# Three of batch 0's activation blocks on GpSimd, and the first batch's loads and products in smaller pieces

## The chip, the cores and the metric

The kernel runs on one core of a Trainium2 chip. Its engines work side by side, each through its own queue in order: TensorE (PE, with its weight loads PEld), VectorE (DVE), ScalarE (ACT), GpSimd (POOL) and SyncE (SP), whose queue issues transfers. GpSimd and ScalarE issue transfers too. The metric is the device time of one execution in microseconds (us).

## The reference

For each of 8 batches and 8 heads, 512 tokens `x` and 32 states `state` of width 64 attend to each other, both ways. The rows of both, heads side by side, then go through a two-layer network with a parametric ReLU:

```python
scores = scale * np.matmul(x, state.transpose(0, 1, 3, 2))
...
xread = np.matmul(a, state)
scores2 = scale * np.matmul(state, x.transpose(0, 1, 3, 2))
...
sread = np.matmul(a2, x)
return np.concatenate([xread, sread], axis=2).astype(np.float32)

h = x @ w_in
g = np.maximum(h, 0.0) + alpha * np.minimum(h, 0.0)
return (g @ w_out).astype(np.float32)
```

`a` and `a2` are softmaxes of the scores. There are 4352 rows, 512 wide; the hidden width is 2048.

## The kernel before

The token rows never form `xread`. A batch's states are multiplied by `w_in` first (`state_w_in`, token `m.b.f`, one for each quarter f of the hidden width, copied to fp16 by `mo`), and the softmax weights of the batch, transposed, then multiply that product: `first` (L562, token `F.b.jc.k`) makes one block of 128 hidden units by 512 tokens of `h` in PSUM bank k with two matmuls, one for each group g of four heads. `negative` (L618, `N`) writes relu(-h) to SBUF on ScalarE, and `prelu` (L623, `G`) makes the fp16 activation from it and from h, which is still in PSUM, on VectorE: neg * (1 - alpha) + h. Sixteen such blocks make a batch. Numbers 0 to 7 are the token rows of the batches, 8 all state rows together.

Batch 0 then takes the second product directly (`second`, L631, `S.b.q.jc2`: two hidden blocks at a time into the bank of token quarter q, drained by `O`). Batches 1 to 8 take one step of a Strassen scheme: seven products `P.b.p.i.c` (L718) of 4 matmuls per piece, on sums of activations (`U`, L694) and of weights (`W`, L676, needed once), drained by `K` (L737) and `Q` (L752). Most U and all W run on GpSimd ("p" at the end of a token; "a" is ScalarE, "v" VectorE).

Batches 1 to 7 get their weights from scores for all 512 tokens in one two-bank PSUM tile (`sc`, also used by whole m products), a block transpose (`sb`), a maximum (`smax`), a shift on GpSimd (`ssh.p`), an exponential on ScalarE (`sexp`), a sum (`ssum`), a product with the reciprocal (`snorm`) and a transpose back (`wb`, L413). The same scores feed the other direction: maximum (`tm`), shift (`nb`), exponentials (`te`), a transposing transfer (`tt`) and reads (`rd`). Batch 0 is taken another way at the start, when nothing else is there: x comes in two fp32 loads on the SP queue (`load_x0`, L164), one for each group of four heads, and is cast (`x0_cast`, L174, `cx.j.g`), transposed on TensorE (`xt.0.j.g.k`, L296), copied out (`xo.0.j.g`, L304) and multiplied with the states into token-major scores (`token_scores`, L350, `tsc.j.g`); j is the half of the tokens. Maximum, shift, exponential, sum and norm follow for each group, then transposes on TensorE (`at`) and copies (`ao`) to the weights.

Nothing is scheduled by a compiler. The string `ORDER` (L17) is a list of tokens, `name.arguments`, and the loop at L778 calls them one after another. The order on each engine is the order of its tokens, and semaphores between the engines follow from the tiles. A bank number in a token fixes what has to be drained before. `Z.k.n` fills TensorE's queue with n matmuls on a pattern. `wi`, `wo`, `lx`, `lst` issue the loads of weights, x and states from GpSimd's queue; `xd` and `tt` issue transposing transfers from SP's.

## Time and profile before

| | |
|---|---|
| time, median of 3 runs (lowest to highest) | 209.35 us (209.3 to 209.4) |
| the profiled execution, its time | 209.3 us |
| the profiled execution, its span in the trace | 207.2 us |
| granted TensorE clock | 1.0 throughout |
| matmuls of first products, batches 0 to 7 (L568) | 256 |
| matmuls of Strassen products (L726) | 840 |
| activation blocks on VectorE (L624), 128x512 and 128x256 | 128 and 16 |

The span runs from the first to the last record of the trace; the time contains 2.1 us around it. Rows of the profile give a line of the kernel, an engine, an operation, what it writes and reads, and its shape. In rows of the timeline the first number is the start, the second the length, in us from the span's start; "xN" merges N instructions. A matmul's length is modelled, and it overlaps the next one's. What stands in brackets is the idle time ahead on that engine and who ended it.

### The profile page before, as it was taken

To read this page: it belongs to the slowest core of one execution; us is meant where nothing else is said; L and a number is where in the kernel's file an instruction comes from. 1 tells how busy PE (TensorE), PEld (TensorE's weight loads), DVE (VectorE), ACT (ScalarE), POOL (GpSimd) and SP (SyncE) were. 2 spreads that over 40 slices of the span, in tenths; PEclk is the share of its full clock that TensorE was granted. 3 is DMA by queue.
4 is the path that set the end of the run, shared out by engine and by line. 5 is a ranking of instruction groups with operands and counts; after the bars stand their busy time and mean duration, and the time that the engine had idled before them with its cause. 6 is when DMAs were issued, how large, how long until landed. Compare 5 with 4: busy or idle time off the path is not lost.

```text
span 207.2 us, 5043 instructions
## 1 busy us (share of the span) xinstructions
PE 198.9 (96%) x2003; PEld 131.7 (64%) x2003; DVE 182.6 (88%) x277; ACT 148.7 (72%) x298; POOL 144.0 (70%) x87
## 2 busy tenths in 40 slices
...
GB/s 178 223 204 204 206 202 184 116 126 198 92 155 166 175 221 179 38 79 135 252 97 131 214 17 51 55 54 103 0 0 99 6 101 54 0 51 74 48 136 152
DMA packets 45943, 24.74 MB, mean 119 GB/s; under 512 B 24288, under 2 KB 45408, under 8 KB 45920
## 3 DMA queue, kind: packets, MB, share of 16 engines
...
q0 software_dynamic: 12688, 8.62, 29.2%
q8 instruction: 15, 0.25, 0.5%
q10 hardware_dynamic: 272, 0.07, 0.1%
q14 instruction: 8, 0.07, 0.1%
...
## 4 chain that ended last, share of the span: by engine, by line
PE 81%; DVE 14%; issue 1%; DMA 1%; ACT 1%; POOL 0%; DVEq 0%; POOLq 0%; ACTq 0%
PE px L726 23%; PE h L568 23%; PE pv L726 12%; DVE g L624 7%; PE py L726 6%; PE o L638 6%; PE h L577 3%; PE m_ps L519 3%; PE fill L230 2%; DVE mx L381 1%; PE sr_ps L469 1%; DVE r L402 1%; DMA out_dram<-oq 1%; PE sc L316 1%; DVE ts L386 1%
## 5 line engine op out<-in xcount | busy, mean ns | idle before, releaser
L624 DVE SCALAR_TENSOR_TENSOR g<-neg,oma_sb,h 128x512 f16<-128x512 f32 (+1 forms) x144 | 94.5, 710 | 4.3 <-ACT neg L621 3.5
L621 ACT ACTIVATE neg<-h 128x512 f32<-128x512 f32 (+1 forms) x144 | 76.1, 590 | 14.0 <-PE h L568 8.2
L568 PE MATMUL h<-aT,m 128*128 128x512 f16 x256 | 64.5, 379 | 0.7 <-DVE g L624 0.5
L726 PEld LDWEIGHTS <-gsum 128*128 128x128 f16 x480 | 46.6, 98 | 9.6 <-issue 1.0
L568 PEld LDWEIGHTS <-m 128*128 128x128 f16 x256 | 24.1, 98 | 25.1 <-issue 4.3
L726 PEld LDWEIGHTS <-g 128*128 128x128 f16 x360 | 34.9, 98 | 7.3 <-issue 0.9
L705 POOL TENSOR_TENSOR gsum<-g 128x1024 f16<-128x1024 f16 (+1 forms) x14 | 28.7, 2060 | 14.4 <-PE pv L726 14.3
L705 POOL TENSOR_TENSOR gsum<-g,g 128x1024 f16<-128x1024 f16 x11 | 23.4, 2129 | 13.2 <-DVE g L624 13.1
L726 PE MATMUL px<-ws,gsum 128*128 128x256 f16 x240 | 29.8, 273 | 0.0
L742 ACT COPY kept<-px 128x512 f32<-128x512 f32 (+1 forms) x21 | 12.2, 582 | 23.8 <-PE px L726 22.8
L705 POOL TENSOR_TENSOR gsum<-gsum,g 128x1024 f16<-128x1024 f16 x11 | 23.4, 2126 | 3.4 <-DVE gsum L705 2.7
L705 POOL TENSOR_TENSOR gsum<-g,gsum 128x1024 f16<-128x1024 f16 x11 | 23.4, 2131 | 0.3
L545 ACT CAST m<-m_ps 128x512 f16<-128x512 f32 x36 | 19.9, 622 | 2.8 <-PE m_ps L519 2.7
L386 POOL TENSOR_TENSOR ts<-ts,mx 128x1024 f32<-128x1024 f32 x7 | 13.4, 1916 | 9.3 <-DVE mx L381 8.8
L638 PE MATMUL o<-w_out_sb,g 128*128 128x512 f16 x64 | 16.5, 379 | 0.0
L759 DVE TENSOR_TENSOR oq<-pv,kept 128x512 f32<-128x512 f32 (+1 forms) x16 | 10.5, 653 | 6.7 <-ACT kept L742 4.4
L726 PE MATMUL px<-w_out_sb,g 128*128 128x256 f16 x120 | 16.1, 273 | 0.0
L726 PE MATMUL px<-w_out_sb,gsum 128*128 128x256 f16 x120 | 16.1, 273 | 0.0
L726 PE MATMUL py<-w_out_sb,g 128*128 128x256 f16 x120 | 16.1, 273 | 0.0
L726 PE MATMUL pv<-ws,gsum 128*128 128x256 f16 x120 | 15.7, 273 | 0.0
L726 PE MATMUL pv<-ws,g 128*128 128x256 f16 x120 | 15.6, 273 | 0.0
L543 ACT CAST m<-m_ps 128x1024 f16<-128x1024 f32 x12 | 12.5, 1042 | 1.7 <-PE m_ps L519 1.6
...
## 6 DMA issues: line engine op xcount, KB each, us to landing
...
```

The costliest lines, as they stand in the source:

```text
L386: engine(e).tensor_tensor(blocks(cols(live["ts", b], j, S)), blocks(scored(b, j)), over_blocks(cols(live["mx", b], j, S // N)), ALU.subtract,)
L519: nc.tensor.matmul(t[N * k : N * (k + 1), :], st_head(b, h)[64 * r : 64 * r + 64, :], w_in_sb[64 * r : 64 * r + 64, c, 512 * f : 512 * (f ...
L543: copier(e)(m_tile(b, f), t)
L545: copier(e)(m_tile(b, f)[:, g, :], t[g])
L568: nc.tensor.matmul(h.rearrange("p (r j s) -> p r j s", r=2, j=2), ms[b, f][:, g, 128 * j : 128 * (j + 1)], weights(b, g), start=(g == 0), ...
L621: nc.scalar.activation(neg, h, RELU, bias=0.0, scale=-1.0)
L624: nc.vector.scalar_tensor_tensor(g_tile(b, jc), negs.pop((b, jc)), oma_sb[:, jc : jc + 1], hs.pop((b, jc)), ALU.mult, ALU.add,)
L638: nc.tensor.matmul(outs[b, q], g_tile(b, jc)[:, 128 * q : 128 * (q + 1)], w_out_sb[:, jc, :], start=not begun and jc == 2 * jc2, stop=left ...
L705: engine(e).tensor_tensor(t, x(), y(), op)
L726: nc.tensor.matmul(pbanks[b, name][:, i, :], of(b, c)[:, j, 128 * i : 128 * (i + 1)], moving[:, 4 * c + j, :], start=not begun and j == 0, ...
L742: copier(e)(t, pbanks[b, "x"])
L759: nc.vector.tensor_tensor(osb, pbanks[b, name], kept[b, add], ALU.add)
```

## The change

x of batch 0 comes in four loads of two heads each (pairs 0 to 3), three on the SP queue and one, pair 2, on ScalarE's, behind the first states' load, which is now issued first. Their fp32 tiles lie in the ring of buffers "osb" (4 of them). `x0_cast(i, g)`, the transposes, their copies and `token_scores(i, g)` take the pair i of group g with all 512 tokens, where they took one half j of the tokens for all four heads of the group; the number of casts, transposes, copies and score matmuls is the same.

`first_of_group` (token `A.b.jc.g.k`) is one of the two matmuls of `first`; sixteen of them replace `F` for the blocks 0 to 7 of batch 0, each pair starting with the group that its token names first. `kept_h` (`C`) copies h from PSUM to SBUF as fp32 on ScalarE, and `prelu_pool` (`H`) makes the activation from the copy on GpSimd with two operations, min(h, 0) * (1 - alpha) and h minus that. Both tiles come from the ring "osb". C and H replace N and G for batch 0's blocks 5, 8 and 11; the other 141 blocks keep N and G.

The whole order is new. Counted over it: 50 of the U's stand on GpSimd (47 before) and 14 on VectorE (17); all K's are on ScalarE (three were on VectorE); one state read is left on VectorE (four before); the shifts nb of batches 1 and 7 go from ScalarE to VectorE and that of batch 5 the other way; one part of the first states' copy and one copy of transposed x more, and one copy of m more, are on VectorE. The nine fills at the start become seven, and the fill at the very end is gone from there. Tokens of the order are shown up to the middle of batch 0 and at the end.

```diff
 ORDER = """
-stc.0.a stt.0.1 sbd.0.a cx.0.0.v lst xt.0.0.0.2 cx.1.0.v sbd.1.a xt.0.1.0.3 xo.0.0.0.a tsc.0.0.4 xo.0.1.0.v tsc.1.0
-cx.1.1.v Z.5.1 smax.0.0 xt.0.1.1.0 xo.0.1.1.v cx.0.1.a xt.0.0.1.2 ssh.v.0.0 sto.0.a Z.3.1 tsc.1.1.5 xo.0.0.1.a tsc.0.1
-m.0.0.1.3 sexp.0.0 mo.0.0.a.1 Z.0.1 smax.0.1 ssh.v.0.1 sexp.0.1 wi.1 str.0.2 wi.2 sro.0.a ssum.0.0 lx.1 snorm.p.0.0
-str.1.4 wi.3 sro.1.a ssum.0.1 oma Z.0.1 snorm.v.0.1 wo.1 Z.3.1 Z.5.1 m.0.1.0.3 mo.0.1.a.0 at.0.5 mo.0.1.a.1 at.1.2
-ao.0.v wo.0 ao.1.v mo.0.0.a.0 m.1.0 mo.1.0.v F.0.7.4 N.0.7 G.0.7 F.0.6.0 F.0.2.5 N.0.6 F.0.1.3 G.0.6 N.0.2 m.2.2.2.1
-N.0.1 mo.2.2.v.0 G.0.1 m.1.1 mo.1.1.a F.0.5.4 G.0.2 F.0.4.0 N.0.4 Z.2.1 N.0.5 m.0.2 mo.0.2.a F.0.3.2 F.0.0.3 N.0.0
-G.0.4 G.0.5 Z.5.1 xt.1.1.1.0 xo.1.1.1.v G.0.0 N.0.3 G.0.3 F.0.8.5 N.0.8 xt.1.0.1.4 xo.1.0.1.a wo.2 lx.2 F.0.9.0 N.0.9
-m.0.3 xt.1.1.0.3 G.0.8 xo.1.1.0.v xt.1.0.0.4 xo.1.0.0.v mo.0.3.a mo.2.2.a.1 Z.2.1 m.3.3.2.5 mo.3.3.a.0 sc.1 m.2.0.3.4
-mo.2.0.a.0 mo.2.0.a.1 G.0.9 wo.3 mo.3.3.a.1 F.0.11.1 S.0.1.3.0 sb.1 smax.1 ssh.p.1 S.0.2.3.2 m.2.3.3.4 mo.2.3.a.0
-N.0.11 W.1.0.p F.0.10.5 S.0.1.2 tm.1 S.0.2.2 G.0.11 N.0.10 G.0.10 F.0.12.3 W.1.1.p mo.2.3.a.1 S.0.1.0 F.0.14.4 N.0.12
-G.0.12 nb.1.a sexp.1 F.0.15.1 ssum.1.5 te.1.1 te.1.0 F.0.13.3 N.0.13 tsum.1 S.0.2.1 snorm.v.1 S.0.1.5 S.0.1.4 N.0.15
-m.1.3 mo.1.3.a S.0.1.1 wb.1 G.0.15 S.0.2.5 N.0.14 G.0.14 S.0.2.4 m.1.2 mo.1.2.a G.0.13 S.0.2.0 F.1.1.5 N.1.1 F.1.13.1
...
-U.7.3.1.v K.8.1.v P.7.7.0.1 P.7.7.1.1 U.8.1.0.v U.8.2.0.v K.7.4.a P.7.3.0.0 P.6.3.0.1 U.8.1.1.v P.8.7.0.0.0 Q.7.1.1
-P.7.4.1.0 P.7.4.1.1 P.7.4.0.0 U.7.4.1.v P.7.4.0.1 U.8.2.1.v P.8.6.0.1 Q.7.1.0 P.8.6.0.0 K.8.2.v P.7.3.1.0 P.7.3.1.1
-U.8.4.0.v U.8.3.1.v Q.6.0.1.a P.8.5.0.1 P.8.5.0.0 K.8.4.a P.8.7.0.1 Q.8.1.1 P.8.2.0.1 Q.8.0.0 P.7.3.0.1 U.8.4.1.v
-P.8.4.0.0 P.8.4.0.1 P.8.3.0.0 Q.7.0.1.a Q.8.1.0 P.8.3.0.1 Q.8.0.1.a Z.1.1
+Z.1.1 lst stc.0.a cx.0.0.v xt.0.0.0.2 stt.0.3 xo.0.0.0.v cx.1.0.a xt.0.1.0.4 sbd.1.v cx.1.1.v xt.0.1.1.5 cx.0.1.a
+xt.0.0.1.0 sbd.0.a wi.1 sto.0.a tsc.0.0.1 xo.0.1.1.a xo.0.1.0.v tsc.1.0 Z.2.1 smax.0.0 Z.3.1 ssh.v.0.0 xo.0.0.1.a
+tsc.1.1.4 sexp.0.0 tsc.0.1 smax.0.1 ssh.v.0.1 lx.1 Z.5.1 m.0.0.2.3 mo.0.0.a.0 Z.0.1 str.1.5 mo.0.0.a.1 str.0.1 Z.0.1
+Z.2.1 wi.2 ssum.0.0 sexp.0.1 Z.4.1 sro.0.a snorm.p.0.0 at.0.3 sro.1.a ssum.0.1 wi.3 m.0.1.0.2 mo.0.1.a.1 snorm.v.0.1
+at.1.4 wo.1 ao.0.v ao.1.v m.4.0.1.5 mo.0.1.v.0 wo.0 m.1.1 mo.4.0.a.1 A.0.3.0.3 mo.4.0.a.0 A.0.1.1.2 A.0.1.0 A.0.2.1.4
+mo.1.1.v A.0.2.0 wo.2 N.0.2 A.0.3.1 N.0.3 lx.2 A.0.5.0.5 A.0.5.1 C.0.5 m.1.0 mo.1.0.a oma G.0.2 H.0.5 xt.1.0.0.0 Z.1.1
+xt.1.0.1.1 G.0.3 A.0.0.1.4 N.0.1 xt.1.1.1.5 xo.1.1.1.v A.0.7.0.3 A.0.7.1 N.0.7 A.0.0.0 N.0.0 A.0.4.1.5 xo.1.0.1.v
+G.0.1 wo.3 m.0.2 G.0.7 xo.1.0.0.v A.0.4.0 N.0.4 G.0.4 mo.0.2.a xt.1.1.0.1 xo.1.1.0.v A.0.6.0.2 m.2.0.3.0 A.0.6.1 N.0.6
+mo.2.0.v.0 m.0.3 mo.0.3.a G.0.6 F.0.11.5 C.0.11 H.0.11 mo.2.0.a.1 xd.2 F.0.8.1 sc.1 m.2.3.3.2 mo.2.3.a.0 C.0.8
+mo.2.3.a.1 G.0.0 sb.1 F.0.10.4 smax.1 S.0.2.2.5 tm.1 m.2.2.0.3 mo.2.2.a.0 S.0.2.3 F.0.15.1 mo.2.2.a.1 F.0.9.2 F.0.13.0
+ssh.p.1 nb.1.v S.0.2.0 N.0.15 G.0.15 S.0.1.1.3 N.0.9 N.0.10 G.0.9 S.0.1.0 S.0.1.2 Z.1.1 sexp.1 G.0.10 ssum.1.2
+snorm.v.1 te.1.0 S.0.1.3 F.0.12.1 F.0.14.4 N.0.13 N.0.14 te.1.1 tt.1 S.0.2.5 S.0.1.5 H.0.8 S.0.2.4 S.0.1.4 G.0.14
+m.1.3 wb.1 S.0.2.1 N.0.12 G.0.12 mo.1.3.a m.3.3.2.4 mo.3.3.a.1 G.0.13 m.1.2 W.3.0.p mo.3.3.a.0 F.1.15.4 N.1.15 G.1.15
+tsum.1 F.1.14.2 N.1.14 G.1.14 F.1.1.1 N.1.1 F.1.0.0 S.0.1.6 G.1.1 F.1.6.4 N.1.0 G.1.0 N.1.6 S.0.2.6 G.1.6 F.1.13.2
...
+P.7.4.1.0 N.8.12 P.7.4.0.1 P.7.4.1.1 U.8.3.1.p P.7.3.1.1 N.8.15 G.8.12 G.8.15 U.8.1.1.v U.8.2.1.v P.7.4.0.0 U.8.2.0.v
+Q.7.1.0 K.8.1.a P.8.6.0.1 P.8.6.0.0 K.8.2.a P.8.7.0.1.5 Q.6.0.1.a P.7.3.0.1 P.8.5.0.0 P.7.3.1.0 P.8.5.0.1 U.8.3.0.p
+P.8.7.0.0 P.8.2.0.0.4 P.8.2.0.1 K.8.4.a Q.8.1.1 P.8.4.0.0 P.8.4.0.1 Q.7.0.1.v U.8.4.0.p P.8.3.0.0 Q.8.0.0 Q.8.1.0
+U.8.4.1.p P.8.3.0.1 Q.8.0.1.a
 """
...
         )
 
 
-    def load_x0(g):
-        if g == 0:
+    def load_x0(pair, queue):
+        if pair == 0:
             xgs["first"] = att.tile([128, H, 2, 2, D], F16, name="xg_first", tag="xg", bufs=3)
-        t = att.tile([128, 4, 2, 2, D], F32, name=f"x0_{g}", tag="ts", bufs=2)
+        t = moe.tile([128, 2, 2, 2, D], F32, name=f"x0_{pair}", tag="osb", bufs=4)
         x0s.append(t)
-        nc.sync.dma_start(
+        queue.dma_start(
             t.rearrange("p k j r d -> p k (j r d)"),
-            x[0, 4 * g : 4 * g + 4].rearrange("k (p t) d -> p k (t d)", t=4),
-        )
-
-    def x0_cast(j, g, e):
-        copier(e)(xgs["first"][:, 4 * g : 4 * g + 4, j, :, :], x0s[g][:, :, j, :, :])
-
-    load_x0(0)
-    load_x0(1)
+            x[0, 2 * pair : 2 * pair + 2].rearrange("k (p t) d -> p k (t d)", t=4),
+        )
+
+    def pair_of_heads(i, g):
+        return slice(4 * g + 2 * i, 4 * g + 2 * i + 2)
+
+    def x0_cast(i, g, e):
+        copier(e)(xgs["first"][:, pair_of_heads(i, g)], x0s[2 * g + i])
+
     rows = state.rearrange("b h n d -> (b h n) d")
     n0 = H * N
     n_j = (B * H * N - n0) // 128
     st0_32 = consts.tile([128, 2, D], F32)
     nc.scalar.dma_start(st0_32, rows[:n0, :].rearrange("(g p) d -> p g d", p=128))
+    load_x0(0, nc.sync)
+    load_x0(1, nc.sync)
+    load_x0(2, nc.scalar)
+    load_x0(3, nc.sync)
     alpha_rows = consts.tile([128, 32], F32)
     nc.vector.memset(alpha_rows, 0.0)
     alpha_quarters = moe_alpha.rearrange("(jc q c) -> q jc c", q=4, c=32)
...
             nc.tensor.matmul(t, pattern[:, :128], pattern, start=True, stop=True)
 
     zs = []
-    fill(0, 9)
+    fill(0, 7)
 
     stT = consts.tile([128, B * H * N], F16)
 
...
         b = b or "first"
         t = live["xp", b, j, g] = single(k, f"xT_ps{b}_{j}_{g}", [128, 4, 128], F16)
         for i in range(4):
-            nc.tensor.transpose(
-                t[:, i, :], xgs[b][:, 4 * g + i, j, :, :].rearrange("p r d -> p (r d)"), ident
-            )
+            if b == "first":
+                block = xgs[b][:, 4 * g + 2 * j + i // 2, i % 2, :, :]
+            else:
+                block = xgs[b][:, 4 * g + i, j, :, :]
+            nc.tensor.transpose(t[:, i, :], block.rearrange("p r d -> p (r d)"), ident)
 
     def x_out(b, j, g, e):
         b = b or "first"
-        copier(e)(x_tile(b)[:, 4 * g : 4 * g + 4, j, :], live.pop(("xp", b, j, g)))
+        t = live.pop(("xp", b, j, g))
+        if b == "first":
+            copier(e)(
+                x_tile(b)[:, pair_of_heads(j, g)].rearrange("p h j s -> p (h j) s"), t
+            )
+        else:
+            copier(e)(x_tile(b)[:, 4 * g : 4 * g + 4, j, :], t)
 
     def scores(b, j=None):
         js = slice(0, 2) if j is None else slice(j, j + 1)
...
         soft_tiles(b)
         nc.vector.transpose(live["ts", b], live["sc", b].rearrange("p r j g s -> p (r j g s)"))
 
-    def token_scores(j, g, k=None):
+    def token_scores(i, g, k=None):
         if ("tsc", g) not in live:
             live["tsc", g] = single(k, f"tsc_{g}", [128, 2, 2, 4, N], F32)
-        for k4 in range(4):
-            h = 4 * g + (k4 ^ g)
-            nc.tensor.matmul(
-                live["tsc", g][:, j, :, k4, :],
-                live["xT", "first"][:, h, j, :],
-                st_pairs[:, h, :, :],
-                start=True,
-                stop=True,
-                skip_group_check=True,
-            )
+        for h in range(8)[pair_of_heads(i, g)]:
+            for j in range(2):
+                nc.tensor.matmul(
+                    live["tsc", g][:, j, :, (h - 4 * g) ^ g, :],
+                    live["xT", "first"][:, h, j, :],
+                    st_pairs[:, h, :, :],
+                    start=True,
+                    stop=True,
+                    skip_group_check=True,
+                )
 
     def tokens_transposed(j, k):
         t = live["at", j] = single(k, f"at_ps{j}", [128, 4, 128], F16)
...
                     stop=(c == n_c - 1),
                 )
 
+    def first_of_group(b, jc, g, k=None):
+        begun = (b, jc) in hs
+        if not begun:
+            hs[b, jc] = single(k, f"h_{b}_{jc}", [128, S], F32)
+        f, j = divmod(jc, 4)
+        nc.tensor.matmul(
+            hs[b, jc].rearrange("p (r j s) -> p r j s", r=2, j=2),
+            ms[b, f][:, g, 128 * j : 128 * (j + 1)],
+            weights(b, g),
+            start=not begun,
+            stop=begun,
+        )
+
     def first_part(b, pair, j, k):
         h = hs[b, pair, j] = single(k, f"h_{b}_{pair}_{j}", [128, 2, S // 2], F32)
         for i in range(2):
...
             g_tile(b, jc), negs.pop((b, jc)), oma_sb[:, jc : jc + 1], hs.pop((b, jc)),
             ALU.mult, ALU.add,
         )
+
+    def kept_h(b, jc):
+        t = negs[b, jc] = moe.tile([128, S], F32, name=f"hsb_{b}_{jc}", tag="osb", bufs=4)
+        nc.scalar.copy(t, hs.pop((b, jc)))
+
+    def prelu_pool(b, jc):
+        h = negs.pop((b, jc))
+        low = moe.tile([128, S], F32, name=f"low_{b}_{jc}", tag="osb", bufs=4)
+        nc.gpsimd.tensor_scalar(low, h, 0.0, oma_sb[:, jc : jc + 1], ALU.min, ALU.mult)
+        nc.gpsimd.tensor_tensor(g_tile(b, jc), h, low, ALU.subtract)
 
     outs = {}
 
...
         "tm": token_max, "nb": token_shift, "te": token_exp, "tsum": token_sum,
         "tt": token_transposed, "rd": state_reads, "rdo": state_reads_out, "rt": reads_turned, "rto": reads_turned_out,
         "m": state_w_in, "mo": state_w_in_out,
-        "F": first, "f": first_part, "n": negative_part, "g": prelu_part, "N": negative, "G": prelu, "S": second, "O": second_out,
+        "F": first, "A": first_of_group, "f": first_part, "n": negative_part, "g": prelu_part, "N": negative, "G": prelu, "C": kept_h, "H": prelu_pool, "S": second, "O": second_out,
         "Z": fill,
         "W": w_sum, "U": g_sum, "P": product, "K": keep, "Q": quarter_out,
     }
```

125 lines of the change are left out of this document (62 added, 63 removed).

## The prediction

> **What bounds the kernel now.** I read the page first, then the chain of waits in order of time, then the timeline of each engine up to 40 us, then the loads of x. The page:
>
> ```profile
> span 207.2 us, 5043 instructions
> ...
> PE 198.9 (96%) x2003; PEld 131.7 (64%) x2003; DVE 182.6 (88%) x277; ACT 148.7 (72%) x298; POOL 144.0 (70%) x87
> ...
> PE 81%; DVE 14%; issue 1%; DMA 1%; ACT 1%; POOL 0%; DVEq 0%; POOLq 0%; ACTq 0%
> ```
>
> TensorE carries most of the chain, but 96% busy is no measure, since a matmul's modelled span overlaps the next one's. So I take the pitch of long runs from the chain of waits (start, length, what):
>
> ```profile
> 33.37 1.38 DVE g L624 x2
> ...
> 46.42 2.59 PE o L638 x12
> ...
> 80.42 2.16 PE h L568 x10
> 82.57 1.75 PE px L726 x16
> ...
> 89.03 0.56 PE m_ps L519 x16
> ...
> 100.17 0.58 PE rt_ps L492 x16
> ...
> 117.43 0.63 PE sr_ps L469 x64
> ...
> 142.32 0.87 PE h L577 x8
> ```
>
> and the first and last rows of the stretch from the timeline, with the scores:
>
> ```profile
> 33.67 1.71 PE L568 MATMUL h<-aT,m 128*128 128x512 f16 x6
> ...
> 52.70 0.41 PE L316 MATMUL sc<-xT,stT 64*32 64x256 f16 x16
> ...
> 202.27 1.04 PE L726 MATMUL px<-w_out_sb,gsum 128*128 128x256 f16 x8
> ```
>
> 33.67 us is batch 1's first product (token F.1.1.5). Behind it in the order stand 224 matmuls of h at 0.216 (48.4 us), 840 of the Strassen products at 0.109 (91.9), 64 of batch 8 at 0.109 (7.0), 40 of the second product at 0.216 (8.6), 20 blocks of m at 0.28 (5.6), seven scores at 0.41 (2.9), eight reads at 0.63 (5.0) and two turns at 0.58 (1.2): 170.6 us. Available are 203.3 - 33.7 = 169.6 us. So from 33.67 us on TensorE is full to within a per cent, and nothing can be gained there. The head has 33.67 us for some 20 us of TensorE work. **The end is the time of batch 1's first product plus the work still left then, plus any new stall.**
>
> What sets 33.67? VectorE's timeline:
>
> ```profile
> 7.72 0.69 DVE L381 TENSOR_REDUCE mx<-tsc 128x16 f32<-128x512 f32 x1
> ...
> 10.68 0.68 DVE L402 TENSOR_REDUCE r<-ts 128x16 f32<-128x512 f32 x1
> ...
> 13.42 0.97 DVE L370 COPY aT<-at_ps 128x512 f16<-128x512 f16 x2
> 14.34 1.23 DVE L543 CAST m<-m_ps 128x1024 f16<-128x1024 f32 x1
> ...
> 16.81 0.69 DVE L545 CAST m<-m_ps 128x512 f16<-128x512 f32 x1
> ...
> 20.04 0.42 DVE L306 COPY xT<-xT_ps 128x512 f16<-128x512 f16 x1
> ...
> 23.67 1.25 DVE L348 STREAM_TRANSPOSE ts<-sc 128x1024 f32<-128x1024 f32 x1
> 24.95 1.22 DVE L381 TENSOR_REDUCE mx<-ts 128x32 f32<-128x1024 f32 x1
> 26.08 1.22 DVE L426 TENSOR_REDUCE nb<-sc 128x2 f32<-128x1024 f32 x1
> ...
> 29.28 1.23 DVE L402 TENSOR_REDUCE r<-ts 128x32 f32<-128x1024 f32 x1
> ...
> 30.95 1.22 DVE L406 TENSOR_TENSOR an<-ts,r 128x1024 f16<-128x1024 f32 x1
> 32.20 1.25 DVE L414 STREAM_TRANSPOSE aT<-an 128x1024 f16<-128x1024 f16 x1
> 33.37 7.29 DVE L624 SCALAR_TENSOR_TENSOR g<-neg,oma_sb,h 128x512 f16<-128x512 f32 x11
> ```
>
> It is packed from 7.72 us, and its transpose of batch 1's weights (wb.1) ends at 33.45 us; F.1 needs it. An activation block costs 7.29 / 11 = 0.66 us there. GpSimd's timeline has two rows of the kind that the change adds:
>
> ```profile
> 11.80 1.05 POOL L406 TENSOR_TENSOR an<-ts,r 128x512 f16<-128x512 f32 x1 [6.06 <-DVE r L403]
> ...
> 26.25 1.91 POOL L386 TENSOR_TENSOR ts<-ts,mx 128x1024 f32<-128x1024 f32 x1 [8.77 <-DVE mx L381]
> ```
>
> and ScalarE's comes close behind VectorE's:
>
> ```profile
> 11.34 2.07 ACT L281 COPY stT<-st_ps 128x896 f16<-128x896 f16 x2
> ...
> 14.86 2.07 ACT L621 ACTIVATE neg<-h 128x512 f32<-128x512 f32 x4
> ...
> 22.83 3.32 ACT L545 CAST m<-m_ps 128x512 f16<-128x512 f32 x6
> ...
> 28.19 1.06 ACT L395 ACTIVATE ts<-ts 128x1024 f32<-128x1024 f32 x1
> 29.16 0.67 ACT L443 ACTIVATE e<-sc,nb 128x512 f16<-128x512 f32 x1
> 29.73 0.19 ACT L443 ACTIVATION_READ_ACCUMULATOR e<-sc,nb 128x1 f32 x1
> ...
> 31.62 1.01 ACT L543 CAST m<-m_ps 128x1024 f16<-128x1024 f32 x1
> ```
>
> **The change, part by part, along the new order.** *Loads of x.* The answer on the tile x says:
>
> ```profile
> L175 DVE CAST xg_first<-x x3: 407/417/828, 5.2 to 7.2; 128x512 f16<-128x512 f32 x3
> L169 SPq DMA_DIRECT2D x<-in_x_dram x2: 472/477/482, 0.7 to 1.3; - x2
> ...
> DMA to landing us min/median/max: 4.4/4.9/5.3
> ```
>
> The two halves land at 0.74 + 4.4 = 5.1 and 1.26 + 5.3 = 6.6 us. Four quarters carry the same bytes, so the first lands sooner (estimate 4.4 to 5.0) and the last again near 6.6. The new order puts the last quarter's cast (cx.1.1) and its transposes on TensorE ahead of the first token scores, which now need only two quarters: that gives the early landing back. 6.6 + 0.41 cast + 0.7 for eight transposes + 0.4 for eight score matmuls gives 8.2 us for the first reduction, against 7.72. Bounds: 0.5 earlier if two queues bring the bytes sooner, 0.5 later if the third issue on SP lands its own issue time later. I take 8.2, since one byte count passes one set of engines. The Trainium skill (DMA: Bandwidth & Descriptors, "Issuing engines are not separate DMA queues") says that transfers started by different engines share the 16 DMA engines and interleave; by it the last quarter gains nothing, and the sum stays as it is. The load issued by ScalarE delays its table load by one issue, 0.48 us; ScalarE waits for the state until 4.9 us anyway. The two initial fills fewer lie in the same wait. The alpha rows now queue on SP behind three loads, not two, 0.48 us later, and are wanted past 15 us; the transposing load of batch 2 moves up on SP, where nothing else waits before the outputs.
>
> *To the weights of batch 0.* Four operations of 0.68 follow with no x copy between them, so the first sum starts at 10.95 against 10.68; ScalarE now has two copies of m (0.55 each) ahead of the second exponential, which ends near 12.0; the second sum and norm end at 13.5, and the copies of the weights at 14.45 (before 14.34), since GpSimd's norm (1.05) and the transposes fill the difference. Then m.0.1 (0.69), m.1.1 (1.23) and one-less-alpha (0.43, formerly ahead of the norm): first G at 16.75. On ScalarE two copies of states (2.07 together) end at 14.1; two m blocks (0.4 each with their gap) and five half products of 0.216 on TensorE follow, so ScalarE's first negative starts at 16.05 and ends 0.6 later, in time. The products by head groups let TensorE begin on the first half of the weights; TensorE isn't the bound here, so I cost them at nothing. Without that cover they would be worth one copy, 0.4.
>
> *From there to wb.1.* Before, from 16.81: one copy of m, eleven G's, three x copies and the softmax of batch 1 took until 33.45. After, from 16.75: again one copy of m, eleven G's (7.3), four x copies at 0.34, the softmax, plus batch 1's shift on VectorE (no more than one small operation, estimate 0.2 to 0.5 between the accumulator row's 0.19 and a 0.42 copy; I take 0.35), less a small reciprocal put behind. 16.64 + 0.34 + 0.35 - 0.15 = 17.2, so wb.1 ends at 33.9. The three blocks given to GpSimd save 3 x 0.66 = 2.0 us of VectorE, but before wb.1 only two fewer G's stand on it (eleven against thirteen), and copies, a shift and a later start eat that. The third is saved behind wb.1, where TensorE is full.
>
> *GpSimd's blocks.* H is two operations on 128x512. One of that kind of size took 1.05, the double size 1.91. So H is 2.1; bounds 1.5 (a single-input operation at half price) and 3.8 (both at the double size's price). H.0.11 stands ahead of ssh.p.1, which wb.1 needs. ScalarE gets to C.0.11 after eight negatives or copies at 0.53 and three whole m copies at 1.0 from 16.05, so 0.53 more ends it at 23.9; H ends at 26.0, and VectorE's maximum arrives at 25.8. Shift 1.91 and exponential 1.06 end at 29.0; VectorE reaches the sum at 29.2. So H.0.11 is hidden by 0.2 us. H.0.5 lies in GpSimd's idle 8.77 us; it is also ahead of wo.3, whose rows are wanted only past 30 us. The second products of blocks 8 and 9 wait for H.0.8, which ends near 30.1; five pieces of TensorE work (2.2 us) stand between them and F.1, so they are wanted at 31.7. Behind H.0.8 GpSimd goes on to the w sums; counting 2.13 each (a row of the groups, below), the gsum for P.1.6.1.0 is ready at 56.9 while TensorE's sum reaches it at 58.9: 2 us of cover.
>
> ```profile
> L681 POOL TENSOR_TENSOR ws<-w_out_sb 128x1024 f16<-128x1024 f16 x4 | 8.5, 2126 | 0.0
> ```
>
> *ScalarE behind the exponential.* Two masked exponentials (0.87), negatives 13, 14, 12 (0.53), m.1.3 (1.0) and a half of m.3.3 (0.55) end at 33.85, which frees bank 4 for F.1.15. So both gates open at 33.9: +0.25 against 33.67, and a wait of 0.1 for bank 2 behind it. TensorE has then done thirteen m blocks against twelve: -0.28. **Sum: +0.25 + 0.1 - 0.28 = +0.1 us.** The work left, the products and the tail (last copy, last store) are the same; the last fill dropped from the tail lay beside the store. The remaining order keeps as many U's on GpSimd (50 against 47), each covered by the same sums. The profiled execution took 209.3 with its span of 207.2; the median is 209.35, so 209.4.
>
> **The rivals.** *R1, faster: x lands early and VectorE is relieved.* If the two queues move the quarters faster, everything up to wb.1 comes 0.5 sooner, and if C.0.11 is not late H stays hidden; with the m block already done and 0.7 us less of VectorE backlog behind wb.1 the gain is 0.5 + 0.28 + up to 0.4 of stalls that TensorE has in the head: 208.3. For it: VectorE sets the chain up to 33.4 us and loses 2.0 us of work. Against: other work took its place.
> *R2, slower: H in front of the shift.* The price decides from 2.3 us on: each 0.1 above that delays ssh.p.1, wb.1 and the end by 0.1. At 3.2 us (0.9 over) the end is +1.0: 210.4; at 3.8 the w sums eat their 2 us of cover too. For it: GpSimd needs 1.05 for what VectorE's row of double width does in 1.22. Against: the rows put H at 2.1.
> *R3, slower: the last quarter late.* It lands at 7.1, its transposes block the scores of the quarters that are there: +0.5, 209.9.
> *R4, slower: a stall behind 34 us* by the new places of shifts, transfers or sums, one of some 1.5 us as the order's margins are near: 211.0. For it: today's stretch has no stall to lose, so any shows in full.
>
> **How the numbers follow.** Forecast 0.38 (own range 209.0 to 210.0, from the bounds of x and of the shift), R1 0.33, R2 0.14, R3 0.07, R4 0.08. About 0.2% (0.42 us) is what can be told from no change. Of the forecast's 0.38, 0.02 falls to faster, 0.26 to same, 0.10 to slower; R1 is faster; R2, R3 and R4 are slower. Faster 0.35, same 0.26, slower 0.39. The range takes R1 (208.3, and 0.2 below it) and R4: 208.1 to 211.1.
>
> **What would show it.** In the changed profile: the first maximum on VectorE at 8.2 (x), the copies of the weights ending at 14.4 to 14.5, the first G at 16.7, two GpSimd operations of about 1.05 per H with the shift of batch 1 starting at 26.0, wb.1 ending at 33.9, and h of batch 1 starting within 0.3 us of that. The forecast is wrong if F.1 starts before 33.2 or after 34.5, or if TensorE idles behind it.

## The result, and the profile after

The kernel before ran 209.36 us (median of 20 runs, 209.2 to 210.32), the changed one 211.02 (20 runs, 209.77 to 215.97). The ratio is 1.0062 with a 95% interval of 1.0038 to 1.0086: slower, by some 0.8 to 1.8 us. It leaves out the five runs of the changed kernel that lie more than 1.5% above its shortest. Two things need explaining: that even the shortest runs are above the median before, and that the changed kernel's runs spread over 6.2 us, where 18 of the 20 runs before lie within 0.31. The profiled execution is one of the shorter ones, 209.96 us with a span of 208.2. Its page:

```profile
span 208.2 us, 5038 instructions
...
PE 199.0 (96%) x2001; PEld 132.1 (63%) x2001; DVE 181.4 (87%) x269; ACT 149.4 (72%) x300; POOL 157.2 (76%) x96
...
PE 83%; DVE 10%; DMA 3%; issue 1%; POOL 1%; SPq 0%; ACT 0%; ACTq 0%; DVEq 0%; POOLq 0%
```

GpSimd has taken 13 us more and VectorE only 1.2 less; in the chain VectorE's share fell from 14 to 10%, and DMA's rose from 1 to 3%. VectorE's timeline answers to the rows shown of before:

```profile
7.79 0.69 DVE L395 TENSOR_REDUCE mx<-tsc 128x16 f32<-128x512 f32 x1 [0.49 <-PE tsc L369]
...
13.77 0.42 DVE L384 COPY aT<-at_ps 128x512 f16<-128x512 f16 x1 [0.25 <-PE at_ps L381]
...
24.63 1.22 DVE L395 TENSOR_REDUCE mx<-ts 128x32 f32<-128x1024 f32 x1
25.77 1.22 DVE L440 TENSOR_REDUCE nb<-sc 128x2 f32<-128x1024 f32 x1
27.01 1.64 DVE L449 TENSOR_SCALAR nb<-nb 128x2 f32<-128x2 f32 x1
...
30.54 1.22 DVE L416 TENSOR_REDUCE r<-ts 128x32 f32<-128x1024 f32 x1
...
33.33 0.74 DVE L651 SCALAR_TENSOR_TENSOR g<-neg,oma_sb,h 128x512 f16<-128x512 f32 x1
33.98 1.24 DVE L428 STREAM_TRANSPOSE aT<-an 128x1024 f16<-128x1024 f16 x1
```

From the copied weights to 25.77 us the changed kernel is 0.2 to 0.3 us ahead of the one before. Then a scaling of 256 numbers, nb.1, takes 1.64 us, and batch 1's sum starts at 30.54 instead of 29.28. VectorE hardly pauses: from the copied weights to the end of wb.1 it is busy 20.71 of 21.03 us, where it was 18.95 of 19.06 before. GpSimd's timeline beside it, and two rows of TensorE's:

```profile
23.41 1.98 POOL L663 TENSOR_SCALAR low<-hsb,oma_sb 128x512 f32<-128x512 f32 x1 [2.10 <-ACT hsb L658]
25.48 1.27 POOL L664 TENSOR_TENSOR g<-hsb,low 128x512 f16<-128x512 f32 x1
26.72 1.90 POOL L400 TENSOR_TENSOR ts<-ts,mx 128x1024 f32<-128x1024 f32 x1
28.61 1.99 POOL L663 TENSOR_SCALAR low<-hsb,oma_sb 128x512 f32<-128x512 f32 x1
30.68 1.27 POOL L664 TENSOR_TENSOR g<-hsb,low 128x512 f16<-128x512 f32 x1
31.91 4.21 POOL L718 TENSOR_TENSOR ws<-w_out_sb 128x1024 f16<-128x1024 f16 x2
```

```profile
29.35 0.38 PE L236 MATMUL fill<-pattern 128*128 128x512 f16 x1 [0.98 <-DVE g L651]
...
35.28 1.90 PE L582 MATMUL h<-aT,m 128*128 128x512 f16 x8 [0.34 <-DVE aT L428]
```

An H costs 1.98 + 1.27 = 3.25 us, the shift of batch 1 waits for H.0.11 until 26.72, and nb.1 ends at 28.65, within 0.03 us of the shift's end (26.72 + 1.90 = 28.62). Batch 1's first product starts at 35.28, against 33.67 before.

**A ruler for all runs.** Two times are read from every profile: W, the end of the second copy of batch 0's weights on VectorE (13.77 + 0.42 = 14.19 here, 13.42 + 0.97 = 14.39 before), and F, the start of batch 1's first product. The span is W, plus F minus W, plus the rest. The kernels of the experiments below stand in it already:

| kernel | W | F | F - W | span - F | span | median (runs) |
|---|---|---|---|---|---|---|
| before | 14.39 | 33.67 | 19.28 | 173.5 | 207.2 | 209.36 (209.2 to 210.3) |
| e3_loads_alone | 14.91 | 34.19 | 19.28 | 173.4 | 207.6 | 210.20 (208.4 to 213.3) |
| g5_before_scores_first | 16.88 | 36.15 | 19.27 | 173.8 | 209.9 | 211.10 (208.8 to 214.8) |
| h1_three_loads | 14.44 | 33.71 | 19.27 | 173.5 | 207.2 | 209.36 (209.2 to 209.7) |
| e2_before_nb_dve | 14.60 | 34.75 | 20.15 | 173.4 | 208.1 | 210.16 (210.0 to 210.3) |
| changed | 14.19 | 35.28 | 21.09 | 172.9 | 208.2 | 211.02 (209.8 to 216.0) |
| f1_two_loads | 14.87 | 35.92 | 21.05 | 173.1 | 209.0 | 211.41 (210.8 to 211.9) |
| f2_w_in_later | 14.67 | 35.59 | 20.92 | 173.0 | 208.6 | 210.62 (210.0 to 213.6) |
| f3_last_quarter_behind | 14.79 | 35.87 | 21.08 | 172.9 | 208.8 | 211.72 (210.5 to 212.2) |
| e1_nb_act | 14.08 | 34.90 | 20.82 | 172.9 | 207.8 | 212.23 (209.6 to 213.0) |
| f4_two_loads_nb_act | 15.38 | 36.18 | 20.80 | 172.9 | 209.1 | 210.98 (210.4 to 211.5) |
| g3_scores_first | 17.13 | 37.77 | 20.64 | 173.0 | 210.8 | 211.59 (209.6 to 215.4) |
| g2_block8_on_vector | 14.12 | 38.54 | 24.42 | 173.1 | 211.6 | 216.10 (213.4 to 219.9) |
| e4_no_gpsimd_blocks | 16.28 | 42.59 | 26.31 | 172.8 | 215.4 | 217.47 (215.7 to 220.2) |

F - W belongs to the order: 19.27 to 19.28 wherever the order before runs from batch 0's products on, 21.05 to 21.09 in the changed kernel, f1 and f3, which leave its order behind W as it is (20.92 in f2, which issues a weight load later). W belongs to the loads and what stands around them. So the change did three things in the profiled run: W -0.20, F - W +1.81, the rest -0.6, together +1.0 on the span, which is the 208.2 - 207.2 measured. In the time that is only 0.6 (209.96 against 209.36), since the time contains 1.8 us around this span and 2.1 around that of before; what shrank there, and what shortened the rest, wasn't taken apart.

### The profile page after: what moved, and what is told of

Same layout as the page of the kernel before. It is cut to its first block, busy times and chain, and to the rows that moved or that the text cites. A ratio compares the mean times of both kernels' runs of the same rounds, so it can differ in the third digit from the quotient of the medians.

```text
span 208.2 us, 5038 instructions
## 1 busy us (share of the span) xinstructions
PE 199.0 (96%) x2001; PEld 132.1 (63%) x2001; DVE 181.4 (87%) x269; ACT 149.4 (72%) x300; POOL 157.2 (76%) x96
## 4 chain that ended last, share of the span: by engine, by line
PE 83%; DVE 10%; DMA 3%; issue 1%; POOL 1%; SPq 0%; ACT 0%; ACTq 0%; DVEq 0%; POOLq 0%
PE px L763 25%; PE h L582 24%; PE pv L763 12%; PE py L763 6%; PE o L675 4%; PE h L591 3%; PE m_ps L533 3%; DVE g L651 3%; DMA x<-in_x_dram 2%; PE sr_ps L483 1%; DVE mx L395 1%; PE h L604 1%; DMA out_dram<-oq 1%; PE sc L330 1%; DVE r L416 1%; DVE nb L449 1%
## 5 line engine op out<-in xcount | busy, mean ns | idle before, releaser
L651 DVE SCALAR_TENSOR_TENSOR g<-neg,oma_sb,h 128x512 f16<-128x512 f32 (+1 forms) x141 | 92.8, 708 | 3.4 <-ACT neg L648 2.6
L648 ACT ACTIVATE neg<-h 128x512 f32<-128x512 f32 (+1 forms) x141 | 73.7, 583 | 13.7 <-PE h L582 9.6
L582 PE MATMUL h<-aT,m 128*128 128x512 f16 x240 | 59.5, 379 | 0.4 <-DVE aT L428 0.3
L582 PEld LDWEIGHTS <-m 128*128 128x128 f16 x240 | 22.8, 98 | 23.5 <-issue 1.5
L742 POOL TENSOR_TENSOR gsum<-gsum,g 128x1024 f16<-128x1024 f16 x12 | 25.5, 2128 | 15.1 <-DVE gsum L742 13.7
L742 POOL TENSOR_TENSOR gsum<-g 128x1024 f16<-128x1024 f16 (+1 forms) x14 | 27.8, 1995 | 11.3 <-PE pv L763 11.2
L779 ACT COPY kept<-px 128x512 f32<-128x512 f32 (+1 forms) x24 | 13.6, 567 | 26.0 <-PE px L763 25.8
L742 POOL TENSOR_TENSOR gsum<-g,gsum 128x1024 f16<-128x1024 f16 (+1 forms) x14 | 27.7, 1991 | 5.1 <-PE px L763 4.7
L742 POOL TENSOR_TENSOR gsum<-g,g 128x1024 f16<-128x1024 f16 x10 | 21.3, 2131 | 4.1 <-DVE g L651 4.0
L559 ACT CAST m<-m_ps 128x512 f16<-128x512 f32 x35 | 19.2, 605 | 2.5 <-PE m_ps L533 2.3
```

The lines of the kernel that those rows point to most:

```text
L559: copier(e)(m_tile(b, f)[:, g, :], t[g])
L582: nc.tensor.matmul(h.rearrange("p (r j s) -> p r j s", r=2, j=2), ms[b, f][:, g, 128 * j : 128 * (j + 1)], weights(b, g), start=(g == 0), ...
L648: nc.scalar.activation(neg, h, RELU, bias=0.0, scale=-1.0)
L651: nc.vector.scalar_tensor_tensor(g_tile(b, jc), negs.pop((b, jc)), oma_sb[:, jc : jc + 1], hs.pop((b, jc)), ALU.mult, ALU.add,)
L742: engine(e).tensor_tensor(t, x(), y(), op)
L779: copier(e)(t, pbanks[b, "x"])
```

## The experiments

**1. Where the 1.81 us come from: nb.1 and GpSimd.** Batch 1's shift back on ScalarE in the changed kernel, and the other way round in the kernel before:

```diff
 e1_nb_act (changed kernel's order)
-ssh.p.1 nb.1.v S.0.2.0 ... Z.1.1 sexp.1
+ssh.p.1 S.0.2.0 ... Z.1.1 nb.1.a sexp.1
 e2_before_nb_dve (order before)
-tm.1 ... nb.1.a sexp.1
+tm.1 nb.1.v ... sexp.1
```

> The changed kernel with the shift nb of batch 1 back on ScalarE, just ahead of the exponential. Theory A (the 8-byte-wide tensor_scalar on VectorE, 27.01 to 28.65 us, is held until GpSimd's shift ends at 28.62): VectorE goes on to its three blocks at 27.0, the sum of batch 1 then waits only for the exponential (ends 29.72), wb.1 ends near 34.4 instead of 35.22 and the time falls by 0.8, to about 209.2. Theory B (the price of GpSimd's blocks, 3.27 us against my 2.1, sets the end by way of ssh.p.1 alone): wb.1 stays at 35.2 and the time at 210.0. On the spread of the runs (209.8 to 216.0): if TensorE's pause at 28.4 to 29.35, which the same wait causes, is what lowers the granted clock in some runs, these runs agree within 0.5 us; if not, they spread as before.

> The kernel before with one token changed: the shift nb of batch 1 on VectorE, right behind tm.1. Theory A: it starts at 27.3 while GpSimd's shift runs from 26.25 to 28.16, takes about 0.9 us until that ends, and wb.1 and the end come 0.8 to 0.9 later: 210.2. If a tensor_scalar of two columns costs only its own work (0.17 us): 209.4, no change.

The second gives the price alone: 210.16 us against 209.33 in the same set, ratio 1.0038 (1.0025 to 1.0052), all runs within 0.3 us. Its rows on VectorE and on GpSimd:

```profile
27.54 0.85 DVE L434 TENSOR_SCALAR nb<-nb 128x2 f32<-128x2 f32 x1
```

```profile
26.46 1.91 POOL L385 TENSOR_TENSOR ts<-ts,mx 128x1024 f32<-128x1024 f32 x1 [8.76 <-DVE mx L380]
28.33 2.12 POOL L680 TENSOR_TENSOR ws<-w_out_sb 128x1024 f16<-128x1024 f16 x1
```

27.54 + 0.85 = 28.39, again just behind the end of GpSimd's operation (26.46 + 1.91 = 28.37). The instruction that starts 0.83 us before GpSimd's shift ends takes 0.85, and the one that starts 1.61 before it takes 1.64: it is held until GpSimd's operation ends. The changed kernel's answer on the tile nb has the free price, 0.168 us, beside the held one:

```profile
L449 DVE TENSOR_SCALAR nb<-nb x2: 168/902/1636, 27.0 to 121.5; 128x2 f32<-128x2 f32 x2
```

The Trainium skill says this of the engines (SBUF — State Buffer, "Who interferes with whom"): VectorE's second pair of ports is GpSimd's only pair, an instruction takes it whole, `tensor_scalar` can be one that does, and the one that comes later is fully blocked. The rows agree, down to an instruction of two columns.

Not every small operation is held. In the kernel before, a reciprocal of the same 256 numbers took 0.15 us in the middle of GpSimd's weight sums, and the norm behind it 1.22, as all fourteen norms of this size in the two kernels did (1.21 to 1.22), each beside an operation of GpSimd:

```profile
30.82 0.15 DVE L453 RECIPROCAL r<-r 128x2 f32<-128x2 f32 x1
```

```profile
28.13 4.21 POOL L681 TENSOR_TENSOR ws<-w_out_sb 128x1024 f16<-128x1024 f16 x2
```

In the first kernel the sum starts 0.90 sooner (29.64 against 30.54) and wb.1 ends at 34.34, as theory A said, but the first product gains only 0.38, of which 0.11 lies ahead of W:

```profile
29.64 1.23 DVE L415 TENSOR_REDUCE r<-ts 128x32 f32<-128x1024 f32 x1 [0.80 <-ACT ts L408]
```

```profile
31.89 1.04 PE L674 MATMUL o<-w_out_sb,g 128*128 128x512 f16 x4 [1.25 <-POOL g L663]
34.90 1.30 PE L581 MATMUL h<-aT,m 128*128 128x512 f16 x5
```

With one cost taken away, the next one behind it shows. VectorE now waits 0.80 for the exponential, and so for GpSimd's shift, which H.0.11 still holds back; TensorE stands 1.25 us for GpSimd's block 8 (H.0.8) and reaches the first product late. By the ruler the hold is worth 0.27 of the 1.81 here. The shift's end to the sum is back at the 1.12 us of before. What is left, 1.54, is 0.67 more to the shift's start, 0.54 more from the sum to wb.1, where a G stands between, and 0.33 more from wb.1 to the product; no run takes these three apart. The median, 212.23 (ratio 1.0134, 1.0099 to 1.0169), shows nothing of the gain and lies above the changed kernel's: the six runs spread from 209.58 to 212.95. The pause at 28.4 us is gone, so it isn't what spreads them.

**2. Are GpSimd's blocks worth having?** Without them, and with one of them on VectorE:

```diff
 e4_no_gpsimd_blocks
-C.0.5 ... H.0.5 ... C.0.11 H.0.11 ... C.0.8 ... nb.1.v ... H.0.8
+N.0.5 ... G.0.5 ... N.0.11 G.0.11 ... N.0.8 ... nb.1.v G.0.8
 g2_block8_on_vector (nb.1 on ScalarE)
-G.0.10 ssum.1.2 ... H.0.8
+G.0.10 H.0.8.v ssum.1.2
-        nc.gpsimd.tensor_scalar(low, h, 0.0, oma_sb[:, jc : jc + 1], ALU.min, ALU.mult)
+        engine(e).tensor_scalar(low, h, 0.0, oma_sb[:, jc : jc + 1], ALU.min, ALU.mult)
```

> The changed kernel with the blocks 5, 8 and 11 of batch 0 made as the others (ScalarE's negative, VectorE's product), three more on VectorE ahead of wb.1. By the sum of the prediction: 2.0 us more on VectorE, less what the shift wins by starting with the maximum (0.9) and nb by being held for less: wb.1 0.5 to 1.5 later than 35.22, time 210.5 to 211.5. Theory B: the blocks on GpSimd cost more than they bring, wb.1 no later than 35.2 and 210.0 or less.

> The changed kernel with nb.1 on ScalarE, and block 8's activation (its two operations on ScalarE's copy) on VectorE just ahead of batch 1's sum instead of on GpSimd behind the shift. Theory C (TensorE's pause of 1.25 us at 30.6 waits for GpSimd's block 8, which costs 3.27 there and stands behind the shift): the pause is gone, the weight sums on GpSimd start near 28.5 instead of 31.8, first product of batch 1 at 34.6 plus or minus 0.3 against 34.9. Rival: VectorE is full there and the block's time on it (some 1.2 us, 0.8 of them in its wait) moves the sum and the first product to 35.2 or later. Spread of the runs as in the changed kernel, since the loads are as they were.

Both are far slower, 217.47 us (ratio 1.0362, 1.0327 to 1.0397), six over its forecast, and 216.1 (1.0272, 1.022 to 1.0324). The first mixes a late load with its own effect; the load is read in the next experiment. The second is clean up to the block, and VectorE's and GpSimd's timelines show the rival, larger than priced:

```profile
28.98 2.37 DVE L662 TENSOR_SCALAR low<-hsb,oma_sb 128x512 f32<-128x512 f32 x1
31.39 2.49 DVE L663 TENSOR_TENSOR g<-hsb,low 128x512 f16<-128x512 f32 x1
```

```profile
28.95 4.38 POOL L717 TENSOR_TENSOR ws<-w_out_sb 128x1024 f16<-128x1024 f16 x2 [0.20 <-DMA w_out_sb<-in_moe_w_out_dram]
33.41 2.44 POOL L717 TENSOR_TENSOR ws<-w_out_sb,ws 128x1024 f16<-128x1024 f16 x1
```

```profile
33.94 1.89 PE L674 MATMUL o<-w_out_sb,g 128*128 128x512 f16 x4 [3.08 <-DVE g L663]
```

The two operations, 1.2 us by the expectation, take 4.86. They lie beside GpSimd's first two weight sums, 4.38 together, and the second ends 0.55 us behind those (33.88 against 33.33): with all operands in SBUF, VectorE moves at about GpSimd's pace. (The Trainium skill says in the same section, SBUF — State Buffer, "Who interferes with whom", that a `tensor_tensor` with two SBUF inputs contends with GpSimd's reads. The second operation here agrees; the norms above, which have two SBUF inputs too, do not.) TensorE's pause grows from 1.25 to 3.08 us. So the pause in the first experiment did wait for block 8, but freeing GpSimd earlier only let its weight sums collide with VectorE. In e4_no_gpsimd_blocks, too, TensorE's second long pause (3.17 us, to 32.52) waits for VectorE's activations. By the ruler its W is 2.09 later than the changed kernel's and its F - W 5.22 longer; at most 1.7 of the 5.22 is the clock (see 3). So in this order the blocks are better on GpSimd than on VectorE, each time by one profile; what they cost there is the waits of what stands behind them.

**3. What spreads the runs: the loads alone.** The four loads with their casts, transposes and scores by pairs, in the order before:

```diff
+    load_x0(2, nc.scalar)
+    load_x0(3, nc.sync)
 (four loads of two heads instead of two of four; ORDER as before)
-    fill(0, 7)
+    fill(0, 9)
```

> The order of before, run with the changed kernel's loads, casts, transposes and token scores (four loads on two queues, pairs of heads); nine fills. If the early landing is worth something by itself: the first cast starts at 3.8 instead of 5.2, the first maximum on VectorE near 7.0 instead of 7.72, wb.1 0.5 earlier and the time near 208.9. If what is won at the start is lost again in front of the weights of batch 0 (GpSimd's norm, the second exponential, the load of w_in): first maximum earlier, but weights copied at 14.3 as before and 209.35.

F - W is the order's 19.28, to the hundredth, and yet the runs spread from 208.44 to 213.25, with a median of 210.2 (ratio 1.0024, 1.0002 to 1.0046). Neither forecast came: the first maximum starts at 7.98 and W is 14.91, since pair 3 lands at 7.64. So the loads bring the spread with them. What they can do in a run stands in the profile of e4_no_gpsimd_blocks, first VectorE's timeline, then a table of stretches (busy TensorE, its granted clock, DMA share, GB/s):

```profile
8.18 0.43 DVE L178 CAST xg_first<-x 128x512 f16<-128x512 f32 x1 [1.91 <-DMA x<-in_x_dram]
```

```profile
5.00:9.00 4.00, 1.50 (x19) 1.00 1.15 201
9.00:13.00 4.00, 4.00 (x52) 0.57 1.23 198
...
30.00:33.00 3.00, 0.47 (x3) 1.00 1.23 197
33.00:37.00 4.00, 4.00 (x12) 0.57 0.77 142
```

Pair 3, SP's third load, has landed at 8.18 instead of 6.41 us. TensorE runs in order, its transposes stand ahead of the scores, and it idles 2.5 us; then its granted clock is 0.57 for the next 4 us. The second pause, at 30 us, again brings 0.57 for 4 us. TensorE is busy all of these, so up to 1.7 us (4 x 0.43) are lost; how much of it reaches the end isn't shown. The Trainium skill (TensorE: Matmul & The Clock Gate, "HAM oscillation — how this bites in real kernels") puts the limit at gaps of about 3.4 us; the trace shows less to be enough. In f1_two_loads below, TensorE's timeline has pauses of 0.81 and 0.74 us, and the stretches behind them a clock of half:

```profile
5.52 0.40 PE L308 MATMUL xT_psfirst<-ident,xg_first 128*128 128x128 f16 x4 [0.81 <-DVE xg_first L179]
...
7.22 0.68 PE L308 MATMUL xT_psfirst<-ident,xg_first 128*128 128x128 f16 x8 [0.74 <-DVE xg_first L179]
```

```profile
7.00:8.00 1.00, 0.78 (x14) 0.82 1.31 208
8.00:9.00 1.00, 1.00 (x10) 0.50 1.16 207
...
10.00:11.00 1.00, 1.00 (x10) 0.50 1.23 206
```

The measurement decides.

The changed kernel's own 20 runs carry marks of this in their mean clocks: the ten of at most 210.9 us all have 0.996 to 1.0, the three of 215.5 to 216.0 all 0.984, and the five with 0.989 to 0.992 took 211.9 to 213.0. The clock isn't the whole of it: one at 213.03 has 1.0, as have two of e1_nb_act at 212.67 and 212.95 and one of g3_scores_first at 215.35. Only the profiled run of a kernel has a trace, so that those very runs had a late landing is argued, not shown.

**4. Is it the load, or its place in the order?** The changed kernel with two loads, alone and with nb.1 on ScalarE; with GpSimd's first weight load issued later; with pair 3's work behind the scores, in two ways (in the second nb.1 is on ScalarE):

```diff
 f1_two_loads, f4_two_loads_nb_act
-    load_x0(1, nc.sync)
-    load_x0(2, nc.scalar)
-    load_x0(3, nc.sync)
+    load_x0(1, nc.sync)
 (four heads in each, in the ring "ts" as before)
 f2_w_in_later
-    load_w_in(0)
-    make_identity(nc, ident)
+    for _ in range(3):
+        make_identity(nc, ident)
+    load_w_in(0)
 f3_last_quarter_behind
-cx.1.1.v xt.0.1.1.5 ... xo.0.1.0.v tsc.1.0 Z.2.1 smax.0.0
+... xo.0.1.0.v ... tsc.1.0 ... tsc.0.1.4 smax.0.0 cx.1.1.v xt.0.1.1.5
 g3_scores_first
-cx.1.1.v xt.0.1.1.5 ... xo.0.1.0.v tsc.1.0 Z.2.1 smax.0.0
+... xo.0.1.0.v cx.1.1.v ... tsc.1.0 ... tsc.0.1.4 smax.0.0 xt.0.1.1.5
```

> The changed kernel with x of batch 0 loaded as in the kernel before (two loads of four heads on SP, cast from there by pairs); order, products by head groups and GpSimd blocks stay. Theory A (the changed kernel's runs spread from 209.8 to 216.0 us because the third SP load, pair 3, lands anywhere between 6.4 and over 8 us while its transposes and its cast stand ahead of the first scores): the runs lie within 0.6 us of each other, median 210.0 (before plus the 0.6 that the held shift and the late sums cost). Theory B (the spread comes from GpSimd's blocks or the order behind 10 us): spread as in the changed kernel, median 211 or more.

> The changed kernel with GpSimd's first load of w_in issued some 1.6 us later (the identity is made three times ahead of it). Theory A1 (the last quarter is late because the w_in packets share the DMA engines with it): x lands by 5.9 us, no wait over 0.3 us at the cast of pair 3, runs within 0.6 us, median 209.8 to 210.2. Theory A2 (the third load of the queue is late by itself): the cast of pair 3 still waits to between 6.4 and 8.2 us and the runs spread by over 2 us.

> The changed kernel with pair 3's cast, transposes and copy behind the scores of the first group and of pair 2 on each engine; the loads stay. Theory A: first maximum near 6.8 us instead of 7.8, second group's softmax takes the delay alone, runs within 1.5 us of each other instead of 6, median 209.4 to 210.2. Theory B: median 211 or more with the spread as it is.

> As the kernel with two loads, and batch 1's shift nb.1 on ScalarE instead of VectorE. Theory A (the two causes add): 0.4 us below the kernel with two loads, 209.6, runs within 0.6 us. Rival: the shift's hold is hidden once the loads are quiet, and the two kernels are equal.

> The changed kernel with nb.1 on ScalarE and pair 3's transposes behind the scores of pairs 0, 1 and 2 on TensorE; its cast stays on VectorE, behind pair 1's copy. Theory A (pair 3 stands in the way of scores that don't need it): first maximum at 7.3 instead of 7.7 to 7.8, weights copied at 13.7 instead of 14.1 to 14.2, first product of batch 1 as much earlier (34.4). Late landings still block VectorE, so a spread of some 2 us stays. Rival: the second group's scores become the late ones, weights copied at 14.2 or later.

With two loads the 20 runs' spread of 6.2 us becomes 1.15 and 1.07 in six runs each, but the time is not the 210.0 forecast: 211.41 (ratio 1.0095, 1.007 to 1.0119) and 210.98 (1.007, 1.0047 to 1.0093). The halves land at 0.74 + 4.3 and 1.26 + 5.2 us, and this order needs all of x before its first scores, so that W is 14.87 and 15.38; the order before needs only the first half there. Theory A was right that the spread shrinks (0.6 was forecast) and wrong of the time. The two medians differ by 0.43, near the 0.4 that the expectation gave to the hold, but their intervals overlap, and in the profiles F - W falls by 0.25 only.

Issuing the weight load later doesn't help: pair 3's cast still waits to 6.39 us in the profile, and four of twelve runs lie at 211.8 to 213.6 (ratio 1.0057, 1.0035 to 1.0079). But it doesn't clear the weight packets either. The load is issued at 3.23 us instead of 1.35, yet the first packet of GpSimd's queue starts at 5.14 instead of 5.07: the edit moved the issue and hardly the packets. The f3 kernel (211.72, ratio 1.0096, 1.007 to 1.0123) moved the first maximum to 7.22 us, but VectorE then casts pair 3 only behind it (7.83), the second group becomes the late one, and W is 14.79. Its spread of 1.66 us is near theory A's 1.5, its median is theory B's. The g3 kernel's profile caught the latest landing of all:

```profile
9.00 0.43 DVE L178 CAST xg_first<-x 128x512 f16<-128x512 f32 x1 [2.28 <-DMA x<-in_x_dram]
```

W is then 17.13 and the span 210.8, though its shortest runs are 209.56 and 209.62; the median is 211.59 (ratio 1.007, 1.0033 to 1.0108). With so late a landing the profile can't test the order that it was made for.

**5. Which load wanders?** The answers on the tile x give the time from issue to landing; the largest is the last piece's. Before, the changed kernel, g5_before_scores_first and g3_scores_first:

```profile
DMA to landing us min/median/max: 4.4/4.9/5.3
```

```profile
DMA to landing us min/median/max: 3.0/3.9/4.6
```

```profile
DMA to landing us min/median/max: 3.0/3.9/7.0
```

```profile
DMA to landing us min/median/max: 3.0/3.8/7.2
```

Over the nine profiles with a third load on SP the largest is 4.5 to 4.7 us five times, and 5.8, 6.4, 7.0 and 7.2 in the other four; with two loads of four heads on SP it is 5.2 to 5.5 in four profiles.

The packets in the traces say what is late. x passes SP's queue in 768 packets of 1024 bytes. The last of them ends at 5.92 to 6.09 us in the five profiles that land on time, and at 7.22, 7.83, 8.34 and 8.60 in the late ones (e3, e4, g5, g3), 0.35 to 0.47 before the cast starts. So the data is late, not only its completion, and little of it: 12, 43, 26 and 27 packets end behind 6.1 us, none in the five others. These are the rows of SP's queue from 6.1 to 9 us (packets, MB, share of the engines), of the changed kernel and of e4_no_gpsimd_blocks:

```profile
q1 hardware_dynamic: 128, 0.01, 6.6%
```

```profile
q1 hardware_dynamic: 168, 0.05, 11.5%
```

The last eight packets in g3_scores_first start 0.133 us apart, the last eight in f2_w_in_later, on time, 0.042 apart. GpSimd's queue moves weights and states in those microseconds. That its packets come between the late ones on the same engine fits, but the records don't name the engine, so it is argued, not shown.

Two kernels with the order before from batch 0's products on test it, with the first group's scores ahead of pair 3's transposes. In the second, heads 4 to 7 come in one load on ScalarE's queue:

```diff
 both
-stc.0.a ... xo.0.1.0.v tsc.1.0 cx.1.1.v Z.5.1 smax.0.0 xt.0.1.1.0 xo.0.1.1.v cx.0.1.a xt.0.0.1.2
+stc.0.a ... cx.0.1.a xt.0.0.1.0 ... xo.0.1.0.v cx.1.1.v tsc.0.0.4 tsc.1.0 ... tsc.0.1.5 smax.0.0 xt.0.1.1.2 xo.0.1.1.a
 h1_three_loads
-    load_x0(2, nc.scalar)
-    load_x0(3, nc.sync)
+    nc.scalar.dma_start(
+        t.rearrange("p k j r d -> p k (j r d)"), x[0, 4:8].rearrange("k (p t) d -> p k (t d)", t=4)
+    )
```

> The kernel before from its first batch's products on (its order, no GpSimd blocks, no products by head groups), with the four loads and the scores of the first group ahead of pair 3's transposes. If the time from the copied weights to batch 1's first product is the order's own (19.28 us in the kernel before and with the loads alone, 21.05 to 21.09 in the changed one), it is 19.3 here, the weights are copied at 13.7 to 14.2, and the run is 208.4 to 209.2, faster than both kernels, with a spread of 1 to 3 us from the landing. Rival: the weights are copied at 14.8 or later, as with the loads alone, and the time is 209.8 or more.

> The kernel before from its first batch's products on, with the scores of the first group ahead of pair 3's transposes, as the run before it of that kind, but heads 4 to 7 (pairs 2 and 3) in one load on ScalarE's queue, so that SP has two loads of x only. Theory A2 (the third load on SP is the one whose landing wanders, 6.3 to 9.0 us in the profiles): the second half lands by 6.6 us in the profile, the runs lie within 1.2 us, median 208.6 to 209.4, and the first product of batch 1 stands 19.3 us behind the copied weights. Rival A3 (whatever comes last of x wanders, on any queue): a wait of 1 us or more at the cast of pair 3 or 2, a spread of over 3 us, median above 210.

The first spreads over 6.0 us (208.77 to 214.79, ratio 1.0028, 0.9998 to 1.0058); its median of 211.1 misses the 208.4 to 209.2, and its profile caught a landing of 8.81 us. The second spreads over 0.47 (209.19 to 209.66, 11 runs). The late half of x is cast on ScalarE and VectorE at 6.13 and 6.60 us, the weights are copied at 14.02 + 0.42 = 14.44:

```profile
6.60 0.42 DVE L177 CAST xg_first<-x 128x512 f16<-128x512 f32 x1
...
14.02 0.42 DVE L385 COPY aT<-at_ps 128x512 f16<-128x512 f16 x1 [0.16 <-PE at_ps L382]
```

```profile
33.71 1.71 PE L583 MATMUL h<-aT,m 128*128 128x512 f16 x6
```

So it is SP's third load of x, not whatever comes last. What sets that load apart isn't separated: being third on its queue, being one of four loads of x, or its size. The median of h1_three_loads is that of the kernel before (ratio 0.9995, 0.9982 to 1.0009), though. With the loads on time the pieces of x bring nothing: the second group's maximum starts at 9.40 us (9.35 before), on the same last bytes, and the weights of batch 0 wait for that group's softmax. No version here beats the kernel before. The changed order with these three loads wasn't run; by the ruler, an estimate, it would give 14.2 to 14.4 + 21.07 + 172.9, a span of 208.2 to 208.4 and about 210.0 us.

## Why the prediction failed where it did

The median of 211.02 lies inside the range of 208.1 to 211.1 and 1.6 above the forecast of 209.4. That it lies inside is luck: the upper end was put there for R4, and R4 isn't there. By the prediction's own sign the forecast is wrong, since F.1 starts at 35.28 us, behind 34.5.

- **The frame held.** The end is the time of batch 1's first product plus a constant: span - F is 172.8 to 173.1 in all nine kernels of the changed order in the table, whatever happens ahead. The work left shrank by 0.6, more than the 0.28 counted.
- **x and batch 0's weights.** First maximum 7.79 (forecast 8.2), weights 14.19 (14.45), in a run with x on time. This step was 0.3 too dear.
- **The step that failed first: the batch's shift nb.1 on VectorE, "no more than one small operation, estimate 0.2 to 0.5".** It took 1.64, outside its own bounds, against the 0.35 taken. The prediction gave VectorE 17.2 us from the first G to the end of wb.1; it took 18.63 (16.59 to 35.22), and 1.29 of the 1.43 more are this one term. The price of the free instruction, 0.168, was even below the bounds; the sum left out that VectorE's small operation would start while GpSimd was in its shift, and be held. The trace before had it to see, in the one shift that stood on VectorE there (93.54 + 0.48 = 94.02) and GpSimd's operation beside it (91.88 + 2.12 = 94.00). In the order before, the move alone costs 0.8 us (e2_before_nb_dve).

```profile
93.54 0.48 DVE L435 TENSOR_SCALAR nb<-nb 128x2 f32<-128x2 f32 x1
```

```profile
91.88 2.12 POOL L705 TENSOR_TENSOR gsum<-gsum,g 128x1024 f16<-128x1024 f16 x1
```

- **H at 2.1 us.** It took 3.25, inside the bounds of 1.5 to 3.8 and past the 2.3 from which R2 was to decide; the mis-sized term is its `tensor_scalar`, 1.98 against 1.05. H.0.11 ended at 26.75, not 26.0, and the shift started at 26.72. The hold runs to that shift's end, so a late H also lengthens it. From W to the shift's start this is +0.67; the hold of nb.1 adds 0.80 (shift's end to the sum: 1.92 against 1.12); a G ahead of wb.1 adds 0.52 (sum to wb.1: 3.44 against 2.92); TensorE follows 0.16 closer. Together 1.83, the 1.81 of the ruler. R2's own price, +1.0 to 210.4, stands near the profiled run's 209.96, but not by R2's path: the sum didn't wait for the exponential behind the shift (it had ended at 29.72), VectorE came late by itself.
- **R3, the last quarter late, had the right mechanism and the wrong size.** It was given 7.1 us and 209.9; in the profiles it lands anywhere from 6.3 to 9.0, and the pause it makes can also take the clock. The forecast's ground, "one byte count passes one set of engines", fits the landings near 6.4 and the 5.35 to 5.46 us by which 95% of the packets of x had passed in the on-time profiles; it says nothing of the few packets that stay behind in the late ones. The rule cited beside it (transfers share the engines, whoever starts them, and interleave) agrees with the on-time landings and doesn't foresee the others.
- **R1, faster, fell** on its own "against": the weights were 0.2 earlier, but between them and the end of wb.1 VectorE had 1.76 us more to do, not less, nb.1's 1.64 most of it.
- **R4**, a stall behind 34 us, isn't there: the rest is shorter, not longer.

The median of 211.02 is thus put down to two losses: some 0.6 us by the order, seen in the run whose x was on time (209.96 against 209.36), and some 1.06 more by SP's third load. The second is the difference to that one run. Experiments 3 to 5 show that the spread goes with this load; its share of the median no run shows, since the two-load kernels, which have no such spread, also get their weights later.
